# A convolution-and-MLP block on one core: the hand-kept list of all operations is searched anew

## The chip, the core and the metric

The kernel runs on one core of one Trainium2 chip. Its engines each take instructions in order from a queue of their own: TensorE (PE, matrix products and weight loads), VectorE (DVE), ScalarE (ACT), GpSimd (POOL) and SyncE (SP, which here only issues transfers). The metric is the device time of one execution in microseconds, as the median of several runs.

## The reference

The block takes `A_u` of shape [1, 2048, 512] (bf16) and adds two branches to it. The first is a layer norm, then a long convolution per channel whose kernel is built from a state-space model, done with Fourier transforms of length 4096. The second is two layer norms in a row and an MLP with a gelu. Cut to what matters:

```python
def _A_ref(u, A_re, A_im, B_re, B_im, C_re, C_im, log_dt, Dskip):
    dt = jnp.exp(log_dt)[:, None]
    logdA = dt * (A_re + 1j * A_im)                     # [512, 128]
    dB = dt * (B_re + 1j * B_im)
    P = jnp.exp(logdA[:, :, None] * arange(2048))       # [512, 128, 2048]
    K = jnp.einsum("dn,dnl,dn->dl", C_re + 1j * C_im, P, dB).real
    Kf, Uf = rfft(pad(K, 4096)), rfft(pad(u.T, 4096))
    y = irfft(Uf * Kf)[:, :2048]
    return y.T + u * Dskip

def _B_ref(x, w1, b1, w2, b2):                          # 512 -> 1376 -> 512
    return gelu(layernorm(x) @ w1 + b1) @ w2 + b2

h = x + _A_ref(layernorm(x), ...)
h2 = h + _B_ref(layernorm(h), ...)
```

## The kernel before

The kernel is straight-line code of 955 operations; there are no hardware loops. All tiles lie in one SBUF arena `ar`, and all matmul results in four PSUM tiles of 128 x 1024 f32 (`ps`), so the names in the profile are few and the lines tell operations apart. The stages, in the order in which they mostly run:

- Setup: loads of the parameters, conversions, roundings and splits on DVE, ACT and POOL (L591 to L626, L703 to L749, L795). `bexps` (L801) makes sixteen exponentials on ACT. Splits of the phase angles end in small f16 tiles that SP copies to other partitions ("restacks", `ar<-ar` at L554).
- `aexps` (L1000 to L1007): ten PE blocks, each followed by an exponential on ACT.
- `chain` (L1045 to L1072), run four times: PE accumulates phases in a PSUM tile step by step (L1050, L1053 for a first step, L1059), ACT takes the sine of the tile after each step (L1068, 36 in all), and DVE multiplies the sines into the exponentials (L1030, L1072, 26 in all). A step can't write its tile before the sine of the step ahead has read it. The first step of a chain needs the restacked tile `S2`.
- The sums over the 128 states, `kgen` and `kgen4` (L1101, L1102, L1132, L1133); the transforms of the kernel and of the normalized input (`kstage` L1167, L1195, `xspec` L961, `fstage` L981, `lstage` L1214); the products of spectra and the inverse transform (`inverse`, L1243 to L1260), whose results go through transposing DMAs on SP (L1266).
- `tail` (L1325 to L1363): residual, statistics and norms, and transposing DMAs of its own; then the MLP: L1384 on PE with the gelu L1386 on ACT, L1406 on PE with the addition L1408 on DVE, and the output DMAs (L554).

Nothing of this order is left to a runtime. `add` records each operation with the engine or engines that may run it and a cost in microseconds for the planner. `ORDER` is a list of all 955 operation numbers, written out; a negative code `~i` puts operation `i` on the second of its engines. `Sched.run` walks it, keeps a clock for each engine from the costs, gives PSUM tiles to the operations that open one (the tile that came free first), and emits the instructions in that order; dependencies between engines become semaphores. The costs thus don't move an operation, but they choose the PSUM tiles, and one more thing: where the planner believes that PE would be idle for over 0.4 us, it puts in dummy matmuls of 512 columns, "fills" (L1511), up to 24 at a place:

```python
if e == "PE" and self.src <= seen and s - free[e] > 0.4 and fs:
    ...
    while t + (0.2 if clk.warm and clk.end > t else 0.4) < s and n0 < FILLN:
        ...
        d.fn = lambda e, z=z: self.fill(z)
```

Each POOL operation other than a DMA also waits for the last DVE operation ahead of it in the list (the dependency named "turns" at the end of the kernel).

Of the kernel before, what the change touches and what calls it, by code (L numbers as in the profile page):

```python
# [10 lines left out]
ALU = mybir.AluOpType  # L11
# [4 lines left out]
P = 128  # L16
# [106 lines left out]
SZ = {f32: 4, bf16: 2, i32: 4, i16: 2, f16: 2}  # L123
# [42 lines left out]
class VS(V):  # L166
# [235 lines left out]
def c_act(n, ptr=0):  # L402
    return 0.055 + n / 1200.0 + 0.09 * min(ptr, 1) + 0.13 * (ptr > 1)
# [7 lines left out]
def kernel(ctx, tc, A_u, A_A_re, A_A_im, A_B_re, A_B_im, A_C_re, A_C_im, A_log_dt, A_Dskip,  # L411
# [28 lines left out]
    add = S.add  # L440
# [111 lines left out]
    def dma(q, out_fn, in_fn, byts, r, w, pr=None, k=1.0):  # L552
        eng = {"SP": nc.sync, "ACT": nc.scalar, "POOL": nc.gpsimd}[q]
        add(q, 1.0 if q == "POOL" else 0.55, lambda e: eng.dma_start(out_fn(), in_fn()), r=r, w=w, byts=byts * k, pr=pr)  # L554
# [77 lines left out]
    raw = {}  # L632
# [299 lines left out]
    def ustats(b):  # L932
        for s in range(8 * b, 8 * b + 8):
            add("DVE", c_dve(512) + 0.05, lambda e, s=s: dve.bn_stats(st[s].ap(), hs[s].ap()), r=[hs[s]], w=[st[s]], hv=0)
# [618 lines left out]
```

## Time and profile before

| what | value |
| --- | --- |
| time, three runs | 235.02, 235.64 and 235.23 us, median 235.23 |
| profiled execution, span on the chip | 233.8 us (first to last instruction; it lies 1.4 us below the median time) |
| busy PE, DVE, ACT, POOL | 202.3, 174.1, 177.2, 38.2 us |
| fills | 41 matmuls, 11.9 us |
| moved by DMA | 20.33 MB |

The span is what the trace holds; the time of a run also has what lies around it. A row of a timeline begins with its start and its busy time in us, followed by engine, line, operation, the tiles written and read with their shapes, and the count of like instructions in a row. In square brackets stands how long the engine was idle before it and who released it. "SPq" is SP issuing a transfer, which is not counted as busy. Matmul rows overlap a little, since their ends are modelled; distances between starts are firmer than single durations.

### The profile page before, as it was taken

The page shows a single profiled execution, that of the slowest core. Times are in us where ns is not written, and L with a number is a line of the kernel's source. Part 1 is how long each engine was busy: PE and PEld are TensorE (multiplying, and loading weights), DVE is VectorE, ACT ScalarE, POOL GpSimd, SP SyncE. Part 2 cuts the span into 40 slices and gives each one's busy share as a digit, 9 for nine tenths or more (in the row PEclk, how much of TensorE's full clock was granted, in tenths as well). Part 3 has the DMA queues.
Part 4 walks back from the last instruction along what each step waited for, and adds up shares of the span by engine and source line. Part 5 has one row for each costly group of instructions (what it writes and reads, how often), then busy time and mean ns, then how long its engine had stood idle before and what let it go on. Part 6 is the DMA issues. An engine that isn't in the chain of part 4 may idle for free.

```text
span 233.8 us, 6809 instructions
## 1 busy us (share of the span) xinstructions
PE 202.3 (87%) x2865; PEld 108.6 (46%) x2865; DVE 174.1 (74%) x296; ACT 177.2 (76%) x218; POOL 38.2 (16%) x184
## 2 busy tenths in 40 slices
PE   4033878968989999999999899999799999999993
PEld 3010643325666685455774254544344444444551
DVE  4989999999998976799899789899906783021021
ACT  4999899999999999898989899976273206906600
POOL 6534372001243113500000030100000101000000
PEclk9999799999999999999999999999999999999998
DMA  6395120300000156789579800434752053053113
GB/s 169 90 202 113 35 70 3 48 1 3 6 3 6 26 158 193 203 209 296 117 133 141 251 3 0 93 70 78 147 97 50 3 101 67 0 104 79 22 22 67
DMA packets 39246, 20.33 MB, mean 87 GB/s; under 512 B 26738, under 2 KB 37012, under 8 KB 39216
## 3 DMA queue, kind: packets, MB, share of 16 engines
q1 hardware_dynamic: 38510, 19.28, 36.8%
q0 software_dynamic: 256, 0.30, 0.6%
q8 instruction: 22, 0.36, 0.6%
q10 hardware_dynamic: 450, 0.33, 0.5%
q14 instruction: 8, 0.07, 0.1%
HBM read 8.10 MB, written 4.49 MB: 54 GB/s over the span
## 4 chain that ended last, share of the span: by engine, by line
PE 54%; ACT 20%; DMA 12%; DVE 5%; issue 4%; SPq 2%; ACTq 1%; DVEq 0%
PE ps L1384 17%; PE ps L1406 13%; ACT ar L1068 10%; PE ps L1260 5%; DMA ar<-ar 5%; ACT ar L542 4%; DMA ar<-in_A_u_dram 3%; PE ps L961 3%; DMA ar<-AK_d 3%; PE ps L1330 2%; PE ps L1059 2%; PE ps L1132 2%; PE ps L1133 2%; PE ps L981 2%; ACT ar L626 2%
## 5 line engine op out<-in xcount | busy, mean ns | idle before, releaser
L542 ACT CAST ar<-ps 128x1024 bf16<-128x1024 f32 (+4 forms) x74 | 65.0, 946 | 4.7 <-PE ps L1260 1.1
L1386 ACT ACTIVATE ar<-ps,ar 128x512 bf16<-128x512 f32 (+1 forms) x44 | 29.0, 685 | 32.9 <-PE ps L1384 32.1
L1384 PE MATMUL ps<-ar 128*128 128x512 bf16 (+1 forms) x176 | 40.4, 379 | 1.3 <-DMA ar<-ar 1.1
L1406 PE MATMUL ps<-ar 128*128 128x512 bf16 (+3 forms) x187 | 39.7, 367 | 0.0
L1068 ACT ACTIVATE ar<-ps 128x1024 bf16<-128x1024 int16 x36 | 34.8, 1067 | 0.5 <-PE ps L1059 0.3
L1408 DVE TENSOR_TENSOR ar<-ps,ar 128x512 bf16<-128x512 f32 (+1 forms) x17 | 11.0, 657 | 30.9 <-PE ps L1406 30.9
L1243 DVE TENSOR_TENSOR ar<-ar 128x2048 bf16<-128x2048 bf16 x24 | 28.9, 1221 | 2.3 <-PE ps L1260 1.7
L544 DVE CAST ar<-ps 128x1024 bf16<-128x1024 f32 (+5 forms) x25 | 26.6, 1070 | 4.3 <-PE ps L981 1.8
L1384 PEld LDWEIGHTS <-ar 128*128 128x128 bf16 (+1 forms) x176 | 17.0, 100 | 22.1 <-issue 2.1
L1406 PEld LDWEIGHTS <-ar 128*128 128x128 bf16 (+1 forms) x187 | 18.0, 97 | 19.9 <-issue 0.4
L1059 PE MATMUL ps<-ar 128*32 128x512 f16 (+1 forms) x368 | 21.6, 331 | 5.3 <-ACT ar L1068 4.7
L1030 DVE TENSOR_TENSOR ar<-ar 128x2048 bf16<-128x2048 bf16 x21 | 24.7, 1218 | 0.1
L926 POOL TENSOR_TENSOR ar<-ar 128x4 f32<-128x4 f32 (+1 forms) x6 | 8.4, 1404 | 69.4 <-DVE ar L603 49.8
L961 PE MATMUL ps<-ar 128*32 128x512 bf16 x256 | 16.5, 380 | 0.5 <-ACT ar L542 0.4
L1059 PEld LDWEIGHTS <-ar 128*32 128x32 f16 x368 | 9.3, 97 | 14.9 <-issue 12.7
L801 ACT ACTIVATE ar<-ar 128x1024 bf16<-128x1024 f32 x16 | 15.5, 1043 | 0.8 <-DVE ar L613 0.8
L1511 PE MATMUL ps<-ar 128*128 128x512 bf16 x41 | 11.9, 429 | 4.2 <-ACT ar L801 4.0
L1260 PE MATMUL ps<-ar 64*128 64x128 bf16 x448 | 15.1, 217 | 0.4 <-DVE ar L1248 0.3
L1260 PEld LDWEIGHTS <-ar 64*128 64x128 bf16 x448 | 12.7, 94 | 5.9 <-issue 1.9
L619 DVE SCALAR_TENSOR_TENSOR ar<-ar 128x4 f32<-128x4 f32 (+5 forms) x37 | 11.2, 309 | 3.4 <-POOL ar L926 2.9
L981 PE MATMUL ps<-ar 128*32 128x256 bf16 (+1 forms) x256 | 13.3, 327 | 0.4 <-DMA ar<-AK_d 0.3
L603 DVE TENSOR_TENSOR ar<-ar 128x1 f32<-128x1 f32 (+9 forms) x36 | 10.9, 312 | 2.9 <-POOL ar L682 2.4
(118 smaller groups left out, 292.1 us busy)
## 6 DMA issues: line engine op xcount, KB each, us to landing
ar<-in_A_u_dram SPq DMA_DIRECT2D x4, 512.0 KB
AK_d<-ar SPq DMA_DIRECT2D x4, 512.0 KB
ar<-AK_d SPq DMA_DIRECT2D x4, 512.0 KB
out_dram<-ar SPq DMA_DIRECT2D x30, 64.0 KB
ar<-in_B_w_dram SPq DMA_DIRECT2D x4, 344.0 KB
ar<-ar SPq DMA_DIRECT2D x20, 64.0 KB
ar<-in_B_w_dram SPq DMA_DIRECT2D x2, 640.0 KB
AL_d<-ar POOLq DMA_DIRECT2D x8, 36.0 KB, 4.8
```

The lines of the kernel that those rows point to most:

```text
L542: act.copy(out_fn(), in_fn())
L544: dve.tensor_copy(out_fn(), in_fn())
L961: pe.matmul(pst(p)[32 * cg:32 * cg + 32, 512 * z:512 * z + 512], lhsT=BD.ap()[:, 32 * f + 2 - 2 * jl:32 * f + 34 - 2 * jl], rhs=un[2 * (2 ...
L981: pe.matmul(pst(p)[64 * h + z:64 * h + z + 32, w * (k + r):w * (k + r) + w], lhsT=T.ap()[:, f, r, z:z + 32], rhs=rhs(f), start=True, stop= ...
L1030: dve.tensor_tensor(o, o[:, 1].unsqueeze(1).to_broadcast([P] + list(o.shape[1:])), f[:, :, ::-1, ::-1] if rev else f, ALU.mult)
L1059: pe.matmul(pst(p)[32 * g:32 * g + 32, 256 * j:256 * (j + n)].rearrange("p (a b) -> p a b", a=n), lhsT=W2[DELTAS.index(d)].ap(), rhs=S2[g] ...
L1068: add("ACT", c_act(1024), lambda e, o_=o_, i_=i_: act.activation(o_(), i_(), ACT.Sin, scale=SINSC), r=[p, TBL], w=[sc[cs]])
L1243: dve.tensor_tensor(pieces(o).rearrange("p z (a r d) -> p a z r d", a=4, r=2), k, x, ALU.mult)
L1260: pe.matmul(pst(p)[:, 512 * h + 128 * k:512 * h + 128 * k + 128], lhsT=o[z].ap()[rows, k, r, :], rhs=TP[w].ap()[rows, f0 // 2 + k, :], sta ...
L1384: pe.matmul(pst(p)[:fs, 512 * z:512 * z + 512], lhsT=w1s[dc].ap()[:, fc * P:fc * P + fs], rhs=ybuf.ap().rearrange("p (t c) k -> p c t k", ...
L1386: add("ACT", c_act(512, 1), lambda e, p=p, z=z, fc=fc, fs=fs: act.activation(hT.ap()[:fs, fc, :], pst(p)[:fs, 512 * z:512 * z + 512], ACT. ...
L1406: pe.matmul(pst(p)[:, 512 * z + c0:512 * z + c1], lhsT=hT.ap()[:fs, fc, 128 * t:128 * t + 128], rhs=w2s[fc].ap()[:fs, c0:c1], start=(fc == ...
```

## The change

The 955 entries of `ORDER` are replaced by another permutation of the same operations. 29 operations go to the other one of their engines (among them several conversions and casts from ACT to DVE, small memsets and one 512-wide f32 product from DVE to POOL, and four normalizations L1355 from ACT to DVE or back). No operation, tile or transfer is added, removed or altered. The planner's costs change too; they show in the instructions only by the PSUM tiles and by the fills, of which there are now 67 instead of 41. The core of the diff, with one of some seventy rows of numbers on either side:

```diff
 ORDER = [
-    152, 175, 183, 32, 216, 176, 128, 217, 136, 193, 34, 118, 127, 41, 184, 194, 153, 195, 154, 155, 156, 218, 220, 129, -136, 295, 196, 221, 157,
+    161, 128, 173, 162, 142, 144, 145, 163, 218, 277, 220, -43, 32, -286, -279, 196, 219, 197, 198, 221, 224, 267, -284, 225, 199, 200, 275, 201, 164,
...
 def c_act(n, ptr=0):
-    return 0.055 + n / 1200.0 + 0.09 * min(ptr, 1) + 0.13 * (ptr > 1)
+    return 0.085 + n / 1200.0 + 0.09 * min(ptr, 1) + 0.13 * (ptr > 1)
...
-        add(q, 1.0 if q == "POOL" else 0.55, lambda e: eng.dma_start(out_fn(), in_fn()), r=r, w=w, byts=byts * k, pr=pr)
+        add(q, 0.65 if q == "POOL" else 0.55, lambda e: eng.dma_start(out_fn(), in_fn()), r=r, w=w, byts=byts * k, pr=pr)
...
-        add("PE", 0.6, trf, r=[raw[nm], identb], w=[p], new=[p] if n == 0 else [])
+        add("PE", 0.4, trf, r=[raw[nm], identb], w=[p], new=[p] if n == 0 else [])
...
-                add("PE", 0.53 + (0 if gn else 0.44), fn, r=[W2, S2] + ([] if gn else [Wm.part(64, 128), S4[0].part(64, 128)] if kind == "B" else [W4, S4]), w=[p], new=[p] if gn == 0 else [])
+                add("PE", 0.43 + (0 if gn else 0.52), fn, r=[W2, S2] + ([] if gn else [Wm.part(64, 128), S4[0].part(64, 128)] if kind == "B" else [W4, S4]), w=[p], new=[p] if gn == 0 else [])
...
-            add("PE", 0.88, mm, r=[kg, W] + ([("carry", q, g) for g in range(4)] if cp else []), w=ps, new=ps)
+            add("PE", 0.975, mm, r=[kg, W] + ([("carry", q, g) for g in range(4)] if cp else []), w=ps, new=ps)
...
-        add("PE", 1.3, mm, r=[kg, W1], w=[p], new=[p])
+        add("PE", 1.09, mm, r=[kg, W1], w=[p], new=[p])
...
-            add("PE", 0.235 * len(terms), fn, r=(o[:1] if mix else o) + TP, w=[p], new=[p])
+            add("PE", 0.25 * len(terms), fn, r=(o[:1] if mix else o) + TP, w=[p], new=[p])
```

The other costs that change are those of a large POOL conversion of f32, the power on POOL (1.5 to 1.7), the batch-norm statistics (0.05 less), `kgen` (0.14 to 0.132), `kgen4` (0.146 to 0.13), the L1214 block (0.25 to 0.34) and the `tail` block (0.85 to 0.91).

The order of the instructions shows in three places. The first is SP ahead of the chain stage, from the restack that waits for a first split on DVE; `DVE` among the waits is the wait for a split, and `DMAHW` with a number is the wait for an earlier transfer on the same of eight counters. Before:

```order
L554 DMA ar<-ar 64x1x512 [waits DMAHW5_49,DVE_49]
L554 DMA ar<-ar 64x1x512 [waits DMAHW6_49]
L554 DMA ar<-ar 64x1x512 [waits DMAHW7_49]
L554 DMA ar<-ar 64x1x512 [waits DMAHW0_49,DVE_49]
L554 DMA ar<-ar 64x1x512 [waits DMAHW1_49]
L554 DMA ar<-ar 64x1x512 [waits DMAHW2_49]
L554 DMA ar<-ar 64x1x512 [waits DMAHW3_49]
L554 DMA ar<-ar 64x1x512 [waits DMAHW4_49]
L1304 DMA ar<-in_A_Dskip_dram 1x4x32 [waits DMAHW5_49]
```

Now:

```order
L554 DMA ar<-ar 64x1x512 [waits DMAHW5_49,DVE_49]
L554 DMA ar<-ar 64x1x512 [waits DMAHW6_49,DVE_49]
L554 DMA ar<-ar 64x1x512 [waits DMAHW7_49]
L554 DMA ar<-ar 64x1x512 [waits DMAHW0_49]
L554 DMA ar<-ar 64x1x512 [waits DMAHW1_49]
L554 DMA ar<-ar 64x1x512 [waits DMAHW2_49]
L1304 DMA ar<-in_A_Dskip_dram 1x4x32 [waits DMAHW3_49]
L554 DMA ar<-ar 64x1x512 [waits DMAHW4_49]
L554 DMA ar<-ar 64x1x512 [waits DMAHW5_49]
```

The wait for the second split (L619 in the profile) moved from the fourth restack to the second, and a small load stands among the restacks.

The second place is ACT at the start of the chain stage, from the load of the table of sines (L536). L1068 is the sine of a chain step; L626 with 128x512 is the arctangent ahead of it or a sine of a code table, as are the other L626. Before:

```order
L536 ACT_TABLE_LOAD
L626 ACTIVATE ar<-ar 128x512
L1068 ACTIVATE ar<-ps_67 128x4x2x128
L1068 ACTIVATE ar<-ps_66 128x4x2x128
L1068 ACTIVATE ar<-ps_67 128x4x2x128
L626 ACTIVATE ar<-ar 128x1024
L1068 ACTIVATE ar<-ps_66 128x4x2x128
```

Now:

```order
L536 ACT_TABLE_LOAD
L626 ACTIVATE ar<-ar 128x32
L626 ACTIVATE ar<-ar 128x512
L1068 ACTIVATE ar<-ps_65 128x4x2x128
L1068 ACTIVATE ar<-ps_66 128x4x2x128
L626 ACTIVATE ar<-ar 128x32
L1068 ACTIVATE ar<-ps_65 128x4x2x128
```

The 128x1024 conversion moved behind more sines, and two small ones stand earlier.

The third place is PE after the second chain step. In this row of PE before, the last matmul of the third step is followed by the first of six fills:

```order
L1059 MATMUL ps_64<-ar 32x256
L1059 LDWEIGHTS ar
L1059 MATMUL ps_64<-ar 32x256
L1511 LDWEIGHTS ar
L1511 MATMUL ps_65<-ar 128x512
```

Now the fills follow the second step, sixteen of them in a row, and the next step comes after them:

```order
L1059 MATMUL ps_66<-ar 32x256
L1511 LDWEIGHTS ar
L1511 MATMUL ps_64<-ar 128x512
...
L1059 LDWEIGHTS ar
L1059 MATMUL ps_65<-ar 32x512
```

The third step of before (of a chain for the second half of the channels) stands later, and between the following steps there are two fills, or four, at most places.

More of the change, by code (lines that the diff above doesn't have):

```diff
@@ L594, in TS @@
         c = c_dve(n, mode, psum) + (0.08 if isinstance(s1, V) else 0.02)
-        add("DVE" if eng == "DVE" else ("POOL", "DVE"), c if eng == "DVE" else (0.25 + n / 1540.0, c), fn, r=r, w=[o], pr=pr, hv=0 if psum else 9 if eng == "POOL" else 1)
+        add("DVE" if eng == "DVE" else ("POOL", "DVE"), c if eng == "DVE" else (0.25 + n / (1540.0 if SZ[o.dt] < 4 or mode > 1 else 1100.0), c), fn, r=r, w=[o], pr=pr, hv=0 if psum else 9 if eng == "POOL" else 1)
     def PTS(o, i, s1, s2=1.0, op0=ALU.mult, op1=ALU.mult, **k):
@@ L925, in stats @@
         STT(buf[1], buf[2], eps1 / 512.0, buf[1], ALU.mult, ALU.add, n=n, pr=pr)
-        POOL(1.5, lambda: gp.tensor_tensor(buf[3].ap(), buf[1].ap(), mhalf.ap().to_broadcast([P, n]), ALU.pow), r=[buf[1], mhalf], w=[buf[3]], pr=pr)
+        POOL(1.7, lambda: gp.tensor_tensor(buf[3].ap(), buf[1].ap(), mhalf.ap().to_broadcast([P, n]), ALU.pow), r=[buf[1], mhalf], w=[buf[3]], pr=pr)
         TT(buf[5], stv, stv, ALU.add, n=n, aap=sa(1), bap=sa(4), pr=pr)
@@ L933, in ustats @@
         for s in range(8 * b, 8 * b + 8):
-            add("DVE", c_dve(512) + 0.05, lambda e, s=s: dve.bn_stats(st[s].ap(), hs[s].ap()), r=[hs[s]], w=[st[s]], hv=0)
+            add("DVE", c_dve(512), lambda e, s=s: dve.bn_stats(st[s].ap(), hs[s].ap()), r=[hs[s]], w=[st[s]], hv=0)
     ustats(0)
@@ L1102, in fn @@
                                 pe.matmul(o, lhsT=Ai.ap()[:, :, d], rhs=Bi.ap()[:, :, d], start=False, stop=True, tile_position=(0, 32 * g))
-                    add("PE", 0.14 * (hi - lo), fn, r=[Ar, Br, Ai, Bi], w=[p], new=[p] if first else [])
+                    add("PE", 0.132 * (hi - lo), fn, r=[Ar, Br, Ai, Bi], w=[p], new=[p] if first else [])
                     first = False
@@ L1133, in fn @@
                         pe.matmul(o, lhsT=w(Ai), rhs=x(Bi), start=False, stop=True)
-                add("PE", 0.146 * h, fn, r=[EA2, Br, IA2, Bi], w=[p], new=[p] if b == 0 else [], hv=1)
+                add("PE", 0.13 * h, fn, r=[EA2, Br, IA2, Bi], w=[p], new=[p] if b == 0 else [], hv=1)
             def ofn(j0=j0, h=h):
@@ L1214, in fn @@
                         pe.matmul(pst(p)[64 * h:64 * h + 64, 256 * (k + r):256 * (k + r) + 256], lhsT=T2.ap()[rows, f0 // 4, r, :], rhs=kin.ap()[rows, f0 // 4, :], start=True, stop=True, tile_position=(32 * z, 64 * h))
-            add("PE", 0.25, fn, r=[T2, kin], w=[p], new=[p])
+            add("PE", 0.34, fn, r=[T2, kin], w=[p], new=[p])
             evac(lambda f0=f0: kf[f0:f0 + 4].ap().rearrange("p f (c g i) -> p f g c i", c=2, g=4), lambda p=p: pst(p).rearrange("p (f g c i) -> p f g c i", f=4, g=4, c=2), 1024, [p], [kf[f0:f0 + 4]])
@@ L1330, in fn @@
                             pe.matmul(o[64 * h:64 * h + 64], lhsT=DD.ap()[:, di].rearrange("p a b -> p (a b)"), rhs=rhs, start=(n == 0 and b == 1), stop=(n == len(terms) - 1))
-            add("PE", 0.85, fn, r=[identb, DD] + [hs[8 * b + 4 * sb + 2 * jp + z] for z in range(2)] + ZT0 + (ZT1 if b else []), w=[p], new=[p])
+            add("PE", 0.91, fn, r=[identb, DD] + [hs[8 * b + 4 * sb + 2 * jp + z] for z in range(2)] + ZT0 + (ZT1 if b else []), w=[p], new=[p])
             for z in range(2):
@@ L1339, in tail @@
                     evac(lambda hh=hh: hh.ap(), src, 512, [p], [hh])
-                add("DVE", c_dve(512) + 0.05, lambda e, j=j, hh=hh: dve.bn_stats(st2[8 * b + j].ap(), hh.ap()), r=[hh], w=[st2[8 * b + j]], hv=0)
+                add("DVE", c_dve(512), lambda e, j=j, hh=hh: dve.bn_stats(st2[8 * b + j].ap(), hh.ap()), r=[hh], w=[st2[8 * b + j]], hv=0)
         stats(st2[8 * b + 4 * sb:8 * b + 4 * sb + 4], nb, 4, 1.0 + EPS, EPS * EPS, pr)
```

64 rows, old and new, of the table ORDER are left out of this document.

## The prediction

> **What bounds the kernel now.** I read the page's summary first, then the busy time of each engine by stage, then the chain of waits. The page:
>
> ```profile
> span 233.8 us, 6809 instructions
> PE 202.3 (87%) x2865; PEld 108.6 (46%) x2865; DVE 174.1 (74%) x296; ACT 177.2 (76%) x218; POOL 38.2 (16%) x184
> ```
>
> PE has most work, but the three large engines are full at different times, as the busy time by stage shows (span, then busy time of PE, PEld, DVE, ACT, POOL, then granted clock, DMA share and GB/s):
>
> ```profile
> 24.00:37.00 13.00, 11.37 (x219) 6.69 (x217) 13.00 (x29) 12.80 (x16) 7.57 (x13) 0.88 0.17 43
> 37.00:79.00 42.00, 36.22 (x944) 20.89 (x936) 40.73 (x65) 41.11 (x50) 7.07 (x6) 1.00 0.06 11
> 79.00:146.00 67.00, 64.70 (x1163) 38.51 (x1165) 57.89 (x78) 62.56 (x73) 8.94 (x11) 1.00 0.61 150
> 171.00:230.00 59.00, 58.67 (x296) 27.41 (x294) 20.35 (x44) 24.07 (x37) 2.01 (x2) 1.00 0.28 57
> ```
>
> From 24 to 79 us DVE and ACT are busy 53.7 and 53.9 of 55 us: the chain stage ends when their lists are done. From 79 us PE is the bound. The chain of waits, in order of time, agrees:
>
> ```profile
> 37.18 1.40 PE ps L1511 x6
> ...
> 76.70 1.09 ACT ar L1068
> 77.82 1.24 DVE ar L1072
> ...
> 220.13 9.56 PE ps L1406 x55
> ```
>
> Six fills (L1511) stand on that chain in the chain stage, whose other end is sines (L1068) and the last product (L1072): a fill is work for nothing, and it counts in full when an engine waits behind it. So three terms decide: when the chain stage ends (T1), how much PE idles or fills after it (T2), and what lies behind the last matmul (T3). I work against the span, 233.8; the median of the runs shown, 235.23, lies 1.4 above it, and I add that at the end.
>
> **T1, the chain stage.** Its first matmuls need the restacked S2, which comes by SP from a split on DVE (L619):
>
> ```profile
> 29.02 0.68 DVE L619 SCALAR_TENSOR_TENSOR ar<-ar 128x512 f16<-128x512 f32 x1
> 30.30 2.46 DVE L934 BATCH_NORM_STATS2 ar<-ar 128x6 f32<-128x512 bf16 x4
> 39.71 0.43 DVE L613 TENSOR_SCALAR ar<-ar 128x512 f16<-128x512 f32 x1
> 26.65 0.54 SPq L554 DMA_DIRECT2D ar<-ar  x1
> 29.72 3.10 SPq L554 DMA_DIRECT2D ar<-ar  x5
> 33.76 0.60 PE L1050 MATMUL ps<-ar 64*128 64x512 f16 x2
> 36.03 0.60 PE L1050 MATMUL ps<-ar 64*128 64x512 f16 x2
> 37.11 1.47 PE L1511 MATMUL ps<-ar 128*128 128x512 bf16 x6
> 38.51 1.05 PE L1059 MATMUL ps<-ar 128*32 128x512 f16 x16
> ```
>
> Before, the split ends at 29.70, five DMAs follow it on SP from 29.72 (0.62 us each, with the gap to the next issue 0.64), the last issue ends at 32.82, and PE starts 0.94 us later.
>
> (a) The split comes earlier. On DVE three batch-norm statistics (four take 2.46, so 0.62 each, together 1.9) and two conversions of L593 (0.3 to 0.4 each, like the L613 row) no longer stand ahead of it; a larger conversion (L591, some 0.9 by its widest kind), one that ACT had (L611, on DVE like the L613, 0.43) and small ones do: -1.9 - 0.7 + 0.9 + 0.4 + 0.2, about -1.1, so 28.6 instead of 29.7.
>
> (b) The transfers behind it get more. In the new SP order the transfer that waits for this split stands second instead of fourth, so the three that stood ahead of it queue behind the wait too, with a small Dskip load: eight issues instead of five. 28.6 + 0.1 + 8 x 0.64 + 0.94 = 34.8 for the first chain matmul, 1.0 later than 33.76.
>
> (c) PE then does two chain steps (33.76 to 36.03 before: 2.27), ending at 37.0, and now **sixteen fills** where three steps and six fills stood. The six took 38.51 - 37.11 = 1.40, so 0.22 to 0.23 each; sixteen 3.5, ending at 40.5. The step behind them takes 0.6, and its sine can start at about 41.1.
>
> ```profile
> 36.91 1.92 ACT L1068 ACTIVATE ar<-ps 128x1024 bf16<-128x1024 int16 x2
> 39.18 1.02 ACT L1068 ACTIVATE ar<-ps 128x1024 bf16<-128x1024 int16 x1 [0.35 <-PE ps L1059]
> 40.10 1.05 ACT L626 ACTIVATE ar<-ar 128x1024 bf16<-128x1024 int16 x1
> 41.05 3.76 ACT L1068 ACTIVATE ar<-ps 128x1024 bf16<-128x1024 int16 x4
> 44.69 0.90 ACT L626 ACTIVATE ar<-ar 128x32 bf16<-128x32 int16 x2
> 72.42 0.44 ACT L542 CAST ar<-ps 128x330 bf16<-128x330 f32 x1
> 72.72 1.06 ACT L1068 ACTIVATE ar<-ps 128x1024 bf16<-128x1024 int16 x1
> ```
>
> Before, ACT had done three sines and the large L626 (0.95 to the next start) by 41.05 and began its fourth sine. Now at 41.1 it begins its third: one sine (0.92) and the large L626 are still to come, 1.9 more. Against that, two small L626 (128x32, 0.12 to 0.14 each from start to next start) are done earlier, and two casts like the L542 shown (0.30 to the next start) have gone to DVE: 0.9 less. **ACT's last sine moves by +1.0.** DVE has its own claim: up to the last product it loses 2.6 us of work to later places and to POOL and gains 1.3 from later places and about 2.6 from ACT and POOL (eight operations of 0.1 to 0.45), so +1.3, less 1.0 us that it idled before its last products (the two waits below). ACT decides: T1 = +1.0. The waits in this stage, by engine (what waited for what: total, times, longest):
>
> ```profile
> ACT ar L626 <- DVE ar L603: 1.2, 1, 1.2
> DVE ar L1115 <- ACT ar L542: 0.7, 1, 0.7
> DVE ar L1072 <- ACT ar L1068: 0.3, 1, 0.3
> PE ps L1059 <- ACT ar L1068: 4.7, 12, 1.1
> ```
>
> Bounds. Below: if the eight issues start when the split does and ACT is behind by itself, the sixteen fills lie in a wait that exists anyway (the step behind them must wait for the sine of its own PSUM tile), and ACT's list is only shorter: -1.1, and -2.3 if the 1.2 us in which ACT waited for DVE's L603 goes too. Above: +2.0, if the moved memsets and the product now on POOL hold DVE up. For that there is a row pair:
>
> ```profile
> 16.72 2.66 POOL L1417 MEMSET ar<- 128x3072 bf16 x1
> 17.55 2.11 DVE L613 TENSOR_SCALAR ar<-ar 128x512 f16<-128x512 f32 x1
> ```
>
> The L613 of 0.43 above took 2.11 beside the long memset, 1.7 us lost. One product of 512 f32 (L603, on DVE as long as the L619 shown, 0.68) now runs on POOL and may hold back what stands beside it. The Trainium skill, "SBUF — State Buffer", section "Who interferes with whom", says that a DVE operation in a two-port mode and a GpSimd operation exclude each other for a whole instruction, and that one with two SBUF inputs loses only to a GpSimd operation that reads; the trace agrees with the first (2.11 against 0.43). By that rule the product on POOL, which reads twice, would block nearly anything on DVE, and moving it gains nothing: T1 would be some 0.5 higher. I leave it in the range.
>
> In the first loads, the tiny b1 load now stands third on SP. By these rows (busy time by stretch, and DVE) the loads had mostly landed at 7 us and DVE first used the transposed ones at 8.81; a delay under 1.8 us is covered, so I take 0, and half a microsecond in the upper bound.
>
> ```profile
> 7.00:8.00 1.00, 0.00 (x0) 0.00 (x0) 1.00 (x6) 1.00 (x2) 0.00 (x0) 1.00 0.16 37
> 8.81 1.22 DVE L544 COPY ar<-ps 128x1024 bf16<-128x1024 bf16 x1
> ```
>
> **T2, PE from 79 us on.** PE idled 67.00 - 64.70 = 2.3 us up to 146 and less behind it. These are the pieces that the new list touches:
>
> ```profile
> 109.80 0.62 PE L981 MATMUL ps<-ar 128*32 128x256 bf16 x16 [0.30 <-DMA ar<-AK_d]
> 126.89 1.05 PE L961 MATMUL ps<-ar 128*32 128x512 bf16 x16 [0.42 <-ACT ar L542]
> 166.79 1.04 PE L1384 MATMUL ps<-ar 128*128 128x512 bf16 x4 [1.12 <-DMA ar<-ar]
> ```
>
> An L1260 block of 1.07 us now stands ahead of the L981 that waited 0.30 for its DMA: -0.3. The L961 of the 0.42 has other work ahead: up to -0.4. The transposing DMA behind the 1.12 is fed earlier, since the statistics ahead of it stand about 2.1 us earlier on DVE and four L1355 moved from one engine to the other: it should issue 0.3 to 0.9 earlier, so I take -0.7. Sum **-1.4**, bounds -2.0 and 0 (a wait covered here may open at the next buffer). Two more fills than before lie in this stage, 0.4 us: inside waits, at 0; if the waits are gone, +0.4.
>
> **T3, the tail.**
>
> ```profile
> 225.48 5.69 SPq L554 DMA_DIRECT2D out_dram<-ar x8
> 229.71 0.42 DVE L1408 TENSOR_TENSOR ar<-ps,ar 128x256 bf16<-128x256 f32 x1 [0.51 <-PE ps L1406]
> ```
>
> SP issues its last eight at 0.71 each and ends at 231.17, 1.47 behind the last matmul (220.13 + 9.56). In the new order eleven of them fall in the last stretch, the final two are the half-width ones that each wait for their own addition: I put the last issue at 1.75 behind. **+0.3.**
>
> Sum: +1.0 - 1.4 + 0.3 = **-0.1**, so a span of 233.7 and a time of **235.1**. Differences up to 0.3%, 0.7 us, can't be told from no change in this kernel's measurements. The forecast's own range, from half of T1 and T2 each way, is 234.0 to 236.2.
>
> **The rivals.**
>
> *Faster: the fills are free.* The sixteen fills and the two-fill pieces between the later steps lie in time in which the step waits for the sine of its tile anyway. For it: PE waited 4.7 us for sines in this stage already. Then ACT ends with its shorter list, T1 = -1.1, T2 = -1.4, T3 = +0.3 less what DVE then bounds (+0.3): -2.2 to -2.4, at **232.9**. Against it: the first fills end at 40.5 by the sum above while ACT would be ready by 39.0. It decides from the point where sixteen fills end before ACT's second sine does.
>
> *Slower: what is late stays late.* The waits after 79 us are relative to transfers that start later too when the chain ends later: the AK transfer, the transposing DMA and the evacuations all hang on it. Then T2 is not -1.4 but about 0, the two added fills count 0.4, T1 +1.0 and T3 +0.3: +1.7, **236.9**. For it: the waits in T2 are on DMAs and ACT, not on PE itself. Against it: the L1260 put ahead of the L981 is PE work that is ready. It decides when less than 0.3 of T2 arrives.
>
> *Slower by the clock.* Fewer fills now stand at 16 us (four for eight) and ahead of the chain (two for six). The fills there ran at half pace, and then at full:
>
> ```profile
> 16.23 3.60 PE L1511 MATMUL ps<-ar 128*128 128x512 bf16 x8 [3.95 <-ACT ar L801]
> ```
>
> Eight in 3.6 us is 0.45 each against 0.23 later, with 0.88 granted from 24 to 37 us. If the clock were low at 34.8, the two steps and sixteen fills (5.8) would take up to twice that: T1 + 5.8 at most, and +2.9 if the clock comes back half way: 238. The Trainium skill, "TensorE: Matmul & The Clock Gate", "What's actually happening", lets the clock fall after a window of about 3.4 us without work and rise after one with it. By that rule and the rows it would not: PE is busy 11.4 of 13 us there. I give it 4%.
>
> *The list does nothing.* The corrected costs concern operations with slack, and every stage ends as before: 235.2, inside the forecast's range.
>
> **How the numbers follow.** Forecast 0.33, list does nothing 0.05, free fills 0.32, late stays late 0.26, clock 0.04. Of the forecast's own range (234.0 to 236.2 about 235.1) a fifth lies below 234.5 and a fifth above 235.9; so faster 0.32 + 0.06 = 0.38, same 0.30, slower 0.26 + 0.04 + 0.02 = 0.32. The range reaches from the free fills with a little more of T2 (232.4) to late stays late with part of the POOL bound (237.2); the clock and the ends of both tails are left out.
>
> **What would show it.** Of T1: in the timeline of SP the last restack issue at 33.8 instead of 32.8, on PE the first L1050 at 34.8 and sixteen fills from 37.0, on ACT a wait of about 2 us behind its second sine, and the last sine ending at 78.8 instead of 77.8. If the fills start later than ACT's second sine or no idle time stands behind it, the faster rival holds. Of T2: the waits of 0.30 and 0.42 gone, the 1.12 below 0.5, and PE from its first L1132 to its last matmul in 149.2 us instead of 150.6 (77.82 + 1.24 to 229.69); 150.6 or more is the slower rival. Of T3: the last SP issue ending 1.75 behind the last matmul. The forecast is wrong if T1 and T2 have the same sign.

## The result, and the profile after

The new list is **slower**: 239.00 us (median of four runs, 238.38 to 239.19) against 235.17, a ratio of 1.0156 with a 95% interval of 1.014 to 1.0173. The forecast of 235.1 and its range, which ended at 237.2, were both wrong. The profiled run took 238.86 us and has a span of 237.1, 3.3 longer than before. In every run whose span is known the time lies 1.7 to 2.1 us above it, so the profile before, with a span of 233.8, belongs to a run of at least 235.5 us; that is why the spans differ by less than the median times, which are 3.8 apart. Runs of one and the same kernel differ, by up to 4.6 us (e1 below), so every kernel is judged by its ratio to the kernel before, run beside it.

The page of the new kernel, and its busy time by stretch (length, busy time of PE, PEld, DVE, ACT, POOL, then granted clock, DMA share and GB/s):

```profile
span 237.1 us, 6841 instructions
PE 205.9 (87%) x2877; PEld 110.7 (47%) x2891; DVE 177.6 (75%) x305; ACT 172.8 (73%) x208; POOL 37.3 (16%) x185
...
36.00:42.00 6.00, 5.95 (x35) 2.08 (x28) 5.83 (x22) 2.70 (x6) 2.46 (x3) 0.72 0.00 0
42.00:62.00 20.00, 19.54 (x248) 6.59 (x248) 16.92 (x21) 19.03 (x22) 0.00 (x0) 1.00 0.06 15
```

and the same stretches before:

```profile
36.00:42.00 6.00, 5.30 (x58) 2.06 (x54) 5.86 (x14) 5.64 (x8) 0.40 (x2) 1.00 0.00 0
42.00:62.00 20.00, 16.97 (x398) 9.05 (x397) 19.86 (x31) 19.91 (x26) 2.33 (x3) 1.00 0.10 16
```

In the chain stage the roles have changed. From 42 to 62 us PE is now busy 19.5 of 20 us, though it finishes fewer matmuls (248 against 398), and DVE has fallen from 19.9 to 16.9. PE paces a stage that DVE and ACT paced before. From 36 to 42 us ACT does 2.7 us of work where it did 5.6, at a granted PE clock of 0.72. The timeline of PE, ACT and DVE in the new kernel shows with what:

```profile
34.35 0.89 PE L1059 MATMUL ps<-ar 128*32 128x256 f16 x16 [1.20 <-DMA ar<-ar]
36.25 5.31 PE L1511 MATMUL ps<-ar 128*128 128x512 bf16 x15
41.49 0.62 PE L1059 MATMUL ps<-ar 128*32 128x512 f16 x8
42.04 0.60 PE L1511 MATMUL ps<-ar 128*128 128x512 bf16 x2
42.58 0.62 PE L1059 MATMUL ps<-ar 128*32 128x512 f16 x8
43.13 0.60 PE L1511 MATMUL ps<-ar 128*128 128x512 bf16 x2
...
42.16 1.02 ACT L1068 ACTIVATE ar<-ps 128x1024 bf16<-128x1024 int16 x1 [3.45 <-PE ps L1059]
47.90 1.67 ACT L626 ACTIVATE ar<-ar 128x512 bf16<-128x512 int16 x2
52.69 11.19 ACT L1068 ACTIVATE ar<-ps 128x1024 bf16<-128x1024 int16 x11 [0.17 <-ACT ar L1068]
63.76 1.14 ACT L626 ACTIVATE ar<-ar 128x1024 bf16<-128x1024 int16 x1
76.72 5.72 ACT L1068 ACTIVATE ar<-ps 128x1024 bf16<-128x1024 int16 x6 [0.80 <-ACT ar L1068]
...
75.54 0.25 PE L1102 MATMUL ps<-ar 128*20 128x33 bf16 x1 [1.06 <-issue]
...
82.47 1.23 DVE L1072 TENSOR_TENSOR ar<-ar 128x2048 bf16<-128x2048 bf16 x1 [0.52 <-ACT ar L1068]
...
83.75 0.29 PE L1132 MATMUL ps<-ar 128*128 128x132 bf16 x1
```

The sixteen fills (one record is missing) run from 36.25 to 41.49, 5.24 us or 0.33 each. Behind them most steps of 0.55 us up to 62 us are followed by two fills of 0.54: 1.09 a step, while ACT needs 0.92 for a sine. Late in the stage, where no fills stand, ACT idles once more, 0.80 us ahead of the sine at 76.72; PE had just stood still for 1.06 us ahead of an L1102 without a wait that the profile shows ("issue"). The kernel before has no such gap there, and what PE stood still for is open. The last product, and with it the first L1132, come 4.65 us later than before (83.75 against 79.10). Behind that point 1.7 us come back up to the last matmul, and the tail loses 0.4:

```profile
223.54 9.07 PE ps L1406 x50
...
227.54 6.96 SPq L554 DMA_DIRECT2D out_dram<-ar  x11
```

The last matmul ends at 232.61, the last issue at 234.50: 1.89 behind it, where it was 1.47.

### The profile page after: what moved, and what is told of

Its sections match the earlier page's. It is cut to its first block, busy times and chain, and to the rows that moved or that the text cites. A ratio compares the mean times of both kernels' runs of the same rounds, so it can differ in the third digit from the quotient of the medians.

```text
span 237.1 us, 6841 instructions
## 1 busy us (share of the span) xinstructions
PE 205.9 (87%) x2877; PEld 110.7 (47%) x2891; DVE 177.6 (75%) x305; ACT 172.8 (73%) x208; POOL 37.3 (16%) x185
## 4 chain that ended last, share of the span: by engine, by line
PE 67%; DVE 12%; ACT 11%; issue 3%; SPq 3%; POOL 1%; DMA 1%; DVEq 0%; POOLq 0%; ACTq 0%
PE ps L1384 16%; PE ps L1406 16%; PE ps L1511 6%; ACT ar L1068 5%; PE ps L1260 5%; PE ps L1059 5%; PE ps L961 4%; PE ps L981 3%; ACT ar L801 3%; PE ps L1330 3%; DVE ar L544 3%; ACT ar L542 2%; SPq L554 2%; PE ps L1132 2%; PE ps L1167 2%
## 5 line engine op out<-in xcount | busy, mean ns | idle before, releaser
L542 ACT CAST ar<-ps 128x1024 bf16<-128x1024 f32 (+3 forms) x73 | 64.7, 947 | 11.6 <-PE ps L1260 6.0
L1384 PE MATMUL ps<-ar 128*128 128x512 bf16 (+1 forms) x176 | 40.4, 379 | 0.6 <-ACT ar L542 0.5
L1068 ACT ACTIVATE ar<-ps 128x1024 bf16<-128x1024 int16 x36 | 35.1, 1033 | 5.1 <-PE ps L1059 3.7
L544 DVE CAST ar<-ps 128x1024 bf16<-128x1024 f32 (+6 forms) x26 | 26.7, 1038 | 6.9 <-PE ps L961 2.1
L1511 PE MATMUL ps<-ar 128*128 128x512 bf16 x60 | 19.2, 432 | 10.0 <-DMA ar<-in_A_u_dram 9.0
L1384 PEld LDWEIGHTS <-ar 128*128 128x128 bf16 (+1 forms) x176 | 17.2, 100 | 21.1 <-issue 2.2
L1059 PE MATMUL ps<-ar 128*32 128x512 f16 (+1 forms) x368 | 21.9, 332 | 1.9 <-DMA ar<-ar 1.2
L926 POOL TENSOR_TENSOR ar<-ar 128x4 f32<-128x4 f32 (+1 forms) x6 | 7.4, 1234 | 84.8 <-DVE ar L619 45.5
L961 PE MATMUL ps<-ar 128*32 128x512 bf16 x256 | 16.0, 380 | 0.1
L1511 PEld LDWEIGHTS <-ar 128*128 128x128 bf16 x67 | 5.7, 106 | 21.0 <-issue 9.6
L1059 PEld LDWEIGHTS <-ar 128*32 128x32 f16 x368 | 8.5, 98 | 12.1 <-issue 9.1
L981 PE MATMUL ps<-ar 128*32 128x256 bf16 (+1 forms) x256 | 13.3, 327 | 0.3 <-ACT ar L542 0.2
```

The source lines that it names most:

```text
L542: act.copy(out_fn(), in_fn())
L544: dve.tensor_copy(out_fn(), in_fn())
L961: pe.matmul(pst(p)[32 * cg:32 * cg + 32, 512 * z:512 * z + 512], lhsT=BD.ap()[:, 32 * f + 2 - 2 * jl:32 * f + 34 - 2 * jl], rhs=un[2 * (2 ...
L1059: pe.matmul(pst(p)[32 * g:32 * g + 32, 256 * j:256 * (j + n)].rearrange("p (a b) -> p a b", a=n), lhsT=W2[DELTAS.index(d)].ap(), rhs=S2[g] ...
L1068: add("ACT", c_act(1024), lambda e, o_=o_, i_=i_: act.activation(o_(), i_(), ACT.Sin, scale=SINSC), r=[p, TBL], w=[sc[cs]])
L1384: pe.matmul(pst(p)[:fs, 512 * z:512 * z + 512], lhsT=w1s[dc].ap()[:, fc * P:fc * P + fs], rhs=ybuf.ap().rearrange("p (t c) k -> p c t k", ...
```

## The experiments

The ratio has a 95% interval; a profile stands for one execution alone. "First L1132" is the end of the chain stage in that profile. e1 to e4 ran on one chip, e5 to e12 on a second, e13 to e16 on a third, each beside the kernel before.

| kernel | ratio to before (95%) | first L1132 | last matmul ends |
| --- | --- | --- | --- |
| before | 1 | 79.10 | 229.7 |
| the new kernel | 1.0156 (1.014 to 1.0173) | 83.75 | 232.6 |
| e1 new, no chain fills | 1.0077 (1.0044 to 1.011) | 80.28 | 230.0 |
| e2 new, only the sixteen | 1.0104 (1.0061 to 1.0146) | 81.03 | 231.1 |
| e3 new, without the sixteen | 1.013 (1.0082 to 1.0177) | 82.71 | 232.1 |
| e4 new, setup fills as before | 1.0103 (1.0067 to 1.014) | 81.80 | 232.5 |
| e5 old, with the new fills | 1.0157 (1.012 to 1.0195) | 82.70 | 232.7 |
| e6 as e1, setup fills as before | 1.0071 (1.0039 to 1.0102) | 79.55 | 229.6 |
| e7 old chain, new rest | 1.0112 (1.0086 to 1.0139) | 80.06 | 229.7 |
| e8 old, no chain fills | 0.9978 (0.9955 to 1.0) | 79.51 | 228.4 |
| e9 new list, old costs | 1.0133 (1.0086 to 1.018) | 82.02 | 233.2 |
| e10 old list, new costs | 1.0025 (0.9995 to 1.0055) | 79.82 | 231.9 |
| e11 old, sixteen for six | 0.9994 (0.9969 to 1.002) | 81.34 | 231.0 |
| e12 as e8, more runs | 0.9943 (0.9916 to 0.9971) | 79.65 | 228.0 |
| e13 new chain, old rest, no chain fills | 1.0019 (0.9979 to 1.0059) | 81.53 | 231.6 |
| e14 old chain, new rest, no chain fills | 1.0089 (1.0053 to 1.0125) | 80.82 | 232.6 |

### Is the chain stage late by its fills?

**e1** leaves out the fills between the third chain step and the tail; **e2** and **e3** leave out one part of them each. The edit is one condition, with other numbers for e2 (`not 224 < i < 400`) and e3 (`i != 224`, where the planner then puts in one fill and 18 of the 32 later ones):

```diff
-            if e == "PE" and self.src <= seen and s - free[e] > 0.4 and fs:
+            if e == "PE" and self.src <= seen and s - free[e] > 0.4 and fs and not 220 < i < 400:
```

> The new list with the 48 fills between the chain steps and ahead of L1167 left out (fills in the setup and from the tail on stay; no operation of the kernel is left out). Theory F, the chain stage is late because PE does fills while ACT and DVE wait: the sine behind the sixteen fills starts at about 39 instead of 42.2, steps follow at ACT's pace, and DVE's list bounds the stage: last product at 79.3 to 79.6 instead of 83.7, time about 234.8 (-4.2). Theory O, the new order of transfers and operations itself makes the chain late: last product still after 82, time 237.5 or more.

> The new list with the sixteen fills kept and the pieces of two and four between later chain steps left out. Theory F: ACT still waits 3.4 us behind its third small conversion, but its later sines follow at 0.92 instead of up to 1.08: last product at about 81.1, time about 236.4 (-2.6). Were the sixteen the whole loss, as the prediction's T1 has it, the time stays at 239. Theory O: 238.5 or more.

> The new list with the sixteen fills left out; the planner then puts in one, and 18 in pieces of two ahead of later steps (32 before). Theory F: the wait of 3.4 us on ACT goes, PE's pace of 1.09 a step binds less: last product at 80.5 to 81, time 235.5 to 236.5. Were the pieces of two the whole loss: 239. Theory O: 238.5 or more.

Without the fills the sine that had waited 3.45 us starts at 38.84 instead of 42.16, and the chain stage ends 3.5 us earlier (80.28), 0.6 to 0.9 later than theory F said. But the time falls only by 1.9 us, to 237.07, not by 4.2. So fills explain three quarters of the stage's delay, and about half of the time; something else in the new list costs the other half.

Each part of the fills alone keeps most of the loss in time. With only the sixteen the stage ends at 81.03, as theory F said, and with only the later pieces at 82.71, though the sine starts at 39.02 there. But by their ratios they take some 237.7 and 238.3 us, above the 236.4 and the 235.5 to 236.5 of theory F and close to the 238.5 of theory O. The delays don't add: the two parts together end the stage at 83.75.

**e5** goes the other way and puts the new pattern of fills into the old list (four and two in the setup, sixteen ahead of the fourth step, two or four ahead of others where a PSUM tile was free). Cut to what matters:

```diff
-FILL0, FILLN = 20.0, 24
+FILL0, FILLN, PAT = 20.0, 24, {185: 4, 218: 2, 226: 16, 224: 2, 232: 2, 230: 4, 238: 2, 236: 2, ...}
...
-            if e == "PE" and self.src <= seen and s - free[e] > 0.4 and fs:
+            if e == "PE" and self.src <= seen and (i in PAT if i < 400 else s - free[e] > 0.4) and fs:
...
-                while t + (0.2 if clk.warm and clk.end > t else 0.4) < s and n0 < FILLN:
+                while n0 < PAT[i] if i < 400 else t + (0.2 if clk.warm and clk.end > t else 0.4) < s and n0 < FILLN:
```

**e11** changes only the six behind the third step to sixteen:

```diff
-                while t + (0.2 if clk.warm and clk.end > t else 0.4) < s and n0 < FILLN:
+                while (n0 < 16) if i == 226 else t + (0.2 if clk.warm and clk.end > t else 0.4) < s and n0 < FILLN:
```

> The old list and costs with the new list's fills: four instead of eight at 16 us, two instead of six ahead of the first chain step, sixteen instead of six behind the third step, then two or four ahead of later steps where a PSUM tile is free for them (34 fills up to the last step; the old list has 32). Theory F, the fills alone make the chain late: the sine behind the sixteen starts at 41.2 (clock full) to 42.9 (clock low) instead of 39.2, last product 2.0 to 3.8 later, time 237.2 to 239.0. Theory O, the order of operations and transfers: within 0.7 us of 235.2.

> The old list and costs with one change: sixteen fills instead of six behind the third chain step. With the clock full the ten more take 2.2 to 2.3 us; the sine behind them starts at 41.3 as in e5 instead of 39.2. Theory F: last product 1.5 to 2.3 later, time 236.7 to 237.5; the rest of e5's +3.6 are the pieces of two. If fills hide in a wait: 235.2 to 235.8.

In the profile of e5, ACT, the last product and its follower:

```profile
41.31 1.02 ACT L1068 ACTIVATE ar<-ps 128x1024 bf16<-128x1024 int16 x1 [2.50 <-PE ps L1059]
...
81.42 1.22 DVE L1072 TENSOR_TENSOR ar<-ar 128x2048 bf16<-128x2048 bf16 x1 [0.32 <-ACT ar L1068]
...
82.70 0.29 PE L1132 MATMUL ps<-ar 128*128 128x132 bf16 x1 [0.23 <-DVE ar L1072]
```

and in that of e11:

```profile
41.33 1.02 ACT L1068 ACTIVATE ar<-ps 128x1024 bf16<-128x1024 int16 x1 [2.51 <-PE ps L1059]
...
80.06 1.22 DVE L1072 TENSOR_TENSOR ar<-ar 128x2048 bf16<-128x2048 bf16 x1 [0.31 <-ACT ar L1068]
81.34 0.29 PE L1132 MATMUL ps<-ar 128*128 128x132 bf16 x1 [0.23 <-DVE ar L1072]
```

Both have the same stall at 41.3, as predicted. e5 ends the stage 3.6 us late and the kernel 3.6 us late (238.72): with no operation moved, the new fills alone make as much loss as the whole change. e11 ends the stage 2.24 late in its profile, where theory F had it, and yet its median is 235.59, no different from before, where the expectation had it for fills that hide in a wait.

How that delay is made up for is shown only in part. In e11's profile the 1.1 us that PE waited for a transposing DMA at L1384 and the 0.4 at L1330 are gone, while the wait for AK_d has grown to 0.9, and the stage behind the chain takes 0.95 us less (81.34 to 230.96, 149.62, against 150.57). But that run was the slowest of ten (236.96). Where the others made up the rest, no profile shows.

### Is it the clock?

**e4** keeps all fills of the new kernel and gives the setup the numbers that the old one has (eight at 16 us, six ahead of the first chain step); **e6** does the same to e1, and **e15** is one more execution of e6, on another chip:

```diff
-                while t + (0.2 if clk.warm and clk.end > t else 0.4) < s and n0 < FILLN:
+                while (t + (0.2 if clk.warm and clk.end > t else 0.4) < s and n0 < FILLN) or n0 < {185: 8, 218: 6}.get(i, 0):
```

> The new list with eight fills at 16 to 20 us and six ahead of the first chain step, as the old one has them (four and two in the new); all other fills stay. Theory C, the clock is low at the sixteen because PE idled ahead of them: granted clock 1.00 there instead of 0.68, sixteen fills in 3.5 to 3.7 us instead of 5.24, time 237.4 (-1.5). If the clock is not what made them slow, they take 5.2 again and the time is 239 or, with four fills too many at 32 us, 239.5.

> The new list without fills from the third chain step to the tail, as e1, and with eight and six fills in the setup, as e4. Theory C (fills ahead of the chain keep the clock up): granted clock near 1.00 from 36 to 42 us instead of e1's 0.56, last product at 79.3 to 79.8 instead of 80.2, time 236.0 to 236.5 against e1's 237.1. If the clock there doesn't matter: as e1.

> The kernel of e6 once more, for its profile: e6's profiled run was the fastest of seven (235.85), the others lay at 236.5 to 237.9. If this run lies there too, the place that differs is a wait on a transfer behind the chain (theory R: at L1330 or L981, 1 to 2 us more idle time of PE), or the clock in the chain stage (theory C: last product 0.5 to 1.5 later).

The busy times by stretch of e4, of e6 and of e15, which is the same kernel as e6:

```profile
36.00:42.00 6.00, 5.95 (x51) 2.11 (x44) 5.83 (x22) 4.24 (x8) 2.59 (x3) 1.00 0.00 0
```

```profile
36.00:42.00 6.00, 2.74 (x44) 0.94 (x34) 5.76 (x22) 6.00 (x10) 2.42 (x3) 1.00 0.00 0
42.00:62.00 20.00, 14.55 (x339) 8.05 (x338) 19.59 (x27) 18.30 (x22) 2.52 (x2) 1.00 0.06 15
```

```profile
36.00:42.00 6.00, 4.00 (x44) 1.24 (x37) 5.79 (x22) 5.99 (x10) 2.45 (x3) 0.66 0.00 0
42.00:62.00 20.00, 16.28 (x308) 7.73 (x307) 19.12 (x26) 18.30 (x22) 1.88 (x2) 0.85 0.06 15
```

In e4 the clock is 1.00, the sixteen fills take 3.6 us, and the time is 238.1: 0.9 of the expected 1.5. But e2, whose fills up to 36 us are those of the new kernel, also shows 1.00 there, and e6 against e15 is one and the same program with 1.00 and with 0.66. So the clock in this stretch is a matter of the single execution; the setup fills are no guarantee, and e6's median (237.42) is that of e1.

e4 and e2 also size the pieces of two at one and the same clock. The stalled sine starts at 40.60 and 40.57, and the stage ends at 81.80 with the pieces and at 81.03 without: 0.8 us. The ratios, 1.0103 and 1.0104, don't differ.

What did the low clock cost? e15 ends the stage 1.42 us later than e6 (80.97 against 79.55) and takes 1.5 us more (237.35 against 235.85); from there to the last matmul both need the same (150.1 and 150.0), so theory R's wait behind the chain isn't what differs. ACT, and two shorter stretches, in e6 and in e15:

```profile
45.44 1.67 ACT L626 ACTIVATE ar<-ar 128x512 bf16<-128x512 int16 x2
50.21 10.20 ACT L1068 ACTIVATE ar<-ps 128x1024 bf16<-128x1024 int16 x11 [0.17 <-ACT ar L1068]
60.24 1.15 ACT L626 ACTIVATE ar<-ar 128x1024 bf16<-128x1024 int16 x1
...
38.00:44.00 6.00, 3.75 (x50) 1.09 (x42) 5.79 (x13) 4.98 (x7) 0.92 (x1) 1.00 0.06 14
52.00:55.00 3.00, 1.90 (x28) 0.68 (x31) 3.00 (x7) 3.00 (x5) 0.00 (x0) 1.00 0.00 0
```

```profile
45.46 1.67 ACT L626 ACTIVATE ar<-ar 128x512 bf16<-128x512 int16 x2
50.24 10.80 ACT L1068 ACTIVATE ar<-ps 128x1024 bf16<-128x1024 int16 x11 [0.17 <-ACT ar L1068]
60.88 1.15 ACT L626 ACTIVATE ar<-ar 128x1024 bf16<-128x1024 int16 x1
...
38.00:44.00 6.00, 5.22 (x48) 1.38 (x40) 5.79 (x13) 5.20 (x7) 0.95 (x1) 0.50 0.05 13
52.00:55.00 3.00, 2.78 (x28) 0.85 (x24) 3.00 (x7) 2.82 (x4) 0.00 (x0) 0.50 0.00 0
```

The low clock from 38 to 44 us costs nothing: at 45.4 both are level. From 52 to 55 us the clock of e15 is 0.50, and its eleven sines take 0.60 longer. The other 0.8 us is lost behind 62 us, where the granted clock is 1.00 in both. So the clock explains 0.6 of the 1.4 us, and what cost the rest is open.

### The costs or the list?

**e9** is the new list with the old costs, **e10** the old list with the new costs.

> The new list with the old costs: the planner then puts fifteen fills ahead of the third chain step instead of sixteen, seven instead of four at 16 us, and no pieces of two between later steps (32 in the new kernel). If the loss is the fills, the new costs made half of it: last product near e2's 79.8 to 81, time 237.0 to 238.0. If the order of operations makes it: 239.

> The old list with the new costs: the planner puts ten fills behind the third step instead of six, two and two instead of six and two later, four as before, nine and three in the setup. Theory F: the sine behind the ten comes 0.9 later than before (4 x 0.23), of which the smaller later pieces give part back: 235.3 to 236.2. If the costs alone make the loss: 238 or more.

e9 puts fifteen fills in one place and none between the later steps, and its profile has the chain stage end at 82.02, at a clock of 0.83 from 36 to 42 us; its time stays at 239.04, against the expected 237 to 238. Without the pieces of two the new list is still slow, as the alternative in the expectation had it. e10 costs 0.7 us against the median before, a little more than expected, and its interval reaches down to no difference. So the costs don't make the loss by themselves.

### The chain part or the rest of the list?

**e7** takes the old list up to its last chain step and the new order for what is left. **e13** and **e14** are the two halves crossed, both without chain fills.

> The old list and costs up to its last chain step, what is left of the operations in the new list's order; fills as in the old list up to there, none ahead of L1132. If T2 of the prediction holds (1.4 us less idle time on PE behind the chain, 0.3 more in the tail): time 234.0 to 234.3. If the waits only change their places, as the idle time of PE in the new kernel says (3.2 us against 3.7, with three fills more): 235.0 to 235.7.

> The new list and costs up to its last chain step, what is left in the old list's order, no fills from the third chain step to the tail. If the new rest is what costs without fills (theory R): the old rest brings it to 234.5 to 235.3, near e8 and e12. If the new chain part costs (theory H): 236.5 to 237.2, as e1.

> The old list and costs up to its last chain step, what is left in the new list's order, no fills from the third chain step to the tail. Theory R: 236.4 to 237.2, two us or more above e12's 234.3. Theory H: 234.3 to 235.0, as e8 and e12.

Where no chain fills are left, the four combinations are: old and old 0.9978 and 0.9943 (e8, e12), new chain and old rest 1.0019, old chain and new rest 1.0089, new and new 1.0077 and 1.0071 (e1, e6). With e7, 1.0112, all four kernels with the new rest lose 0.7 to 1.1%, and their intervals begin at 1.0039 or higher. **Behind the old chain, theory R holds: the new rest costs 1.1 to 1.5% there** (e7 against before, e14 against e8 and e12).

Behind the new chain it is not shown. The interval of e13 overlaps those of e1 and e6. Its median, 237.24 us, is that of e1 and e6, at the upper end of what theory H had; only because the kernel before took 236.78 on that chip is the ratio 1.0019. What the new chain part adds to the old rest is as uncertain: e13's interval lies above that of e12 and overlaps that of e8. So both parts of the list can cost time, and the two costs don't add.

Part of e7's and e14's loss is a seam that no whole list has: DVE work of the new rest stands ahead of the last two products, PE waits 1.09 us ahead of the first L1132, and the stage ends at 80.06 in e7 (before 79.10) and at 80.82 in e14 (e12 79.65). And the cost behind the seam differs between executions. In e14's profile PE needs 3.5 us more from the first L1132 to its last matmul than in e12's (151.8 against 148.3). In that of e7, which is its fastest run (236.01, the others 237.4 to 238.4), it needs 0.9 less than before.

What PE waited for from 79 us on in e14,

```profile
PE ps L1132 <- ACT ar L542: 1.1, 1, 1.1
PE ps L1325 <- ACT ar L542: 0.8, 1, 0.8
PE ps L1330 <- DMA ar<-in_B_b_dram: 0.8, 1, 0.8
```

and in e12, with the old rest,

```profile
PE ps L961 <- ACT ar L542: 0.4, 1, 0.4
PE ps L1260 <- DVE ar L1248: 0.3, 1, 0.3
PE ps L1325 <- ACT ar L542: 0.3, 1, 0.3
```

Of e14's three waits, 2.7 us, e12 has 0.3, and the first of the three is the seam, ahead of the first L1132; e14 has fifteen fills behind 79 us against nine. Both profiles are of runs near their medians, on two chips. That the waits and fills are the whole of it is argued, not shown: none of them was taken away alone.

### The old list without its fills

**e8** and **e12** leave the 18 fills of the chain stage out of the old list, with e1's condition; **e16** is a second profile of the kernel before.

> The old list without its 18 fills from the third chain step on (those of the setup and the tail stay). Theory F alone: fills cost here too, the 0.35 us that ACT waits behind the six goes, time 234.8 to 235.2. Theory C: without them the clock falls in the chain as in e1 (0.56 from 36 to 42 us) and steps take up to twice as long: 235.7 to 236.7.

> The kernel of e8 again, in five rounds, to tell whether leaving the 18 chain fills out of the old list beats both kernels: 234.2 to 234.7 against 235.1 by e8, an interval that ends below 1.000. If e8 was chance: within 0.3 us of the kernel before.

> The kernel before once more, for its profile: its runs lie at 235.1 or at 236.8. If this one lies at 236.8, theory R has PE wait 1 to 2 us more on a transfer behind the chain (L981 or L1384); theory C has the chain stage end later at a lower clock. If it lies at 235.1, the profile repeats the first.

Leaving them out beats both kernels: e12 takes 234.34, a ratio of 0.9943 with an interval that ends at 0.9971; e8's interval ends at 1.0. The chain stage ends half a microsecond later than before (79.65 against 79.10; clock 0.93 to 0.96 from 36 to 62 us), in the direction of theory C, though not at its clock of 0.56, and the time is shorter all the same, since PE waits less behind it: the 1.1 us at L1384 is not in e12's list of waits. e16 came in at 235.22 and repeats the first profile, with first L1132 at 79.10 and a wait of 1.17 at L1384; the times near 236.8 have no profile. Why that transposing DMA is in time when the chain ends later stays open.

## Why the prediction was wrong, point by point

- **T1 (a) and (b), the start of the chain: cancelled out.** The split ended at 27.97, not 28.6, and the eight issues behind it at 33.04, not 33.8, each step 0.63, close to the 0.64 forecast. The timeline of the new kernel:

```profile
27.99 3.10 SPq L554 DMA_DIRECT2D ar<-ar  x5
31.13 0.66 SPq L1304 DMA_DIRECT2D ar<-in_A_Dskip_dram  x1
31.84 1.20 SPq L554 DMA_DIRECT2D ar<-ar  x2
```

  The matmul that needs these transfers is L1059, not the L1050 that the prediction watched: it started at 34.35, against 34.30 before. Both shifts came as forecast, but before, the profile shows no wait for a transfer ahead of that matmul, so there was less for them to move: the net was 0.05 us instead of 1.0.
- **T1 (c), the sixteen fills: right in place, too small.** ACT waits behind its second sine and a small conversion, 3.45 us instead of 2, since the fills took 5.24 us instead of 3.5. The rival "slower by the clock" named this and was given 4%; e1 and e15 show a low clock from 36 to 42 us too (0.56 and 0.66). By the rule of the Trainium skill, "TensorE: Matmul & The Clock Gate", "What's actually happening", as the prediction read it, the clock would not fall behind a stage in which PE is 87% busy. In the new kernel that stage had fewer fills and PE was busy only 9.4 of the 13 us from 24 to 37 us, and the granted clock did fall, though nothing like a whole window without work stands there: the longest gap of PE in that stretch is 1.20 us. So this trace doesn't bear the rule out as the prediction read it; e4 against e2 leaves open how far the setup fills decide it. The prediction took the old kernel's busy share for the new one.
- **T1, the step that failed: its size.** T1 came out at +4.65, not +1.0, outside its own bounds of -2.3 to +2.0. The prediction charged the sixteen fills, at their price with the clock full, and put the other 32 at nothing; they appear only in the faster rival, as fills in time that is idle anyway. e6, the same list with no fills in this stage and a clock of 1.00, shows where the time went. Its stage ends only 0.45 later than before. The other 4.2 us arise at three places. The stall of the sixteen leaves 2.46 (L626 at 47.90 against 45.44); it is less than the 3.45 because without it ACT waits 1.53 for DVE a little later. The pieces of two add 1.06 by 64 us (63.76 against 60.24): the eleven sines among them take 11.19 us in the new kernel, in e3 and in e4, and 10.20 in e2, e6 and e9, which have no pieces there. The last 0.7 comes late in the stage, where no fills stand, and its cause is open.
- **T2, PE behind the chain, the second step that failed: the length came out by luck, the reason fell.** From the first L1132 to the last matmul it took 148.9 us, predicted 149.2, and T1 and T2 have opposite signs, as the prediction asked. The waits of 0.30 and 0.42 that the prediction named at L981 and L961 are indeed gone, and of the 1.12 at L1384 0.5 is left, for another engine. But others stand in their place; what PE waited for from 79 us on:

```profile
PE ps L1325 <- ACT ar L542: 0.8, 1, 0.8
PE ps L1330 <- DMA ar<-in_B_b_dram: 0.7, 1, 0.7
PE ps L1384 <- ACT ar L542: 0.5, 1, 0.5
```

  Where the chain isn't late (e7, e14), the kernel with the new rest is slower by 2.6 to 3.5 us, the seam included, not 1.4 faster. And without fills in the chain the prediction's own terms give the 232.9 of its faster rival; e1 took 237.07, four us more. In e11 an old rest behind a late chain is shorter too. So the gain that the new kernel shows here may come from the chain being late and not from the order: the prediction read from the waits of the old kernel which of them the new list removes, and did not ask which it makes. What in the new order makes them is open.
- **T3, the tail: right.** The last issue ends 1.89 behind the last matmul, predicted 1.75.
- **From the span to the time.** The prediction added 1.4 us, the median time less the span of the profile. But that profile belongs to a run slower than the median, and a run's time lies 1.7 to 2.1 above its own span. The step is some 0.4 us too small, which doesn't decide anything.
- **The rivals.** "The fills are free" fell in e1 and e5; only in e11 did ten more fills leave the median time where it was. "Late stays late" was right in sign, at 236.9 too small by 2.1, and wrong in its mechanism: the stage behind the chain gave time back. "The list does nothing" fell with the result, and in e7 and e14. The chances don't add up as written: with a fifth of the forecast's 0.33 on either side, slower is 0.37 and same 0.25.

## What to carry to other kernels

A dummy instruction is free only while the engine behind it waits for something else: add up a step with its fills and compare the sum with the pace of the engine that consumes it, and count every small group, not the largest one. When an order is searched with a model, the model's own filler depends on its costs: the corrected costs, 0.03 us more for each sine among them, put two fills between most steps where the old costs put none (e9). And a wait that a new order removes says nothing without those that it makes; crossing the two halves of the old and the new list showed a cost that neither profile did, but the seam between the halves has a cost of its own.

## What the runs showed of the hardware

The granted PE clock of one and the same program was 1.00 in one execution and down to 0.50 in another, on another chip, from 38 to 44 and from 52 to 55 us (e6 and e15), though the longest gap of PE between 21 and 58 us is 1.4 us in both. Where ACT was waiting for DVE anyway this cost nothing; from 52 to 55 us it cost 0.6 us. The mean clock of a whole run doesn't tell its time: the kernel before took 234.93 us at 0.981 and 236.88 at 1.000. A stage ahead of the PE-bound part that ended 2.2 us late in the profile left the median time as it was (e11), while one that ended 3.6 us late cost all of it (e5).
